# Sinks and sums of two attention steps handled as one item

## The chip, the cores and the metric

The kernel runs on one core of a Trainium2 chip. The metric is the device time of one execution in microseconds (us); lower is better. The engines of the core are TensorE (PE in the profile; PEld is its weight load), VectorE (DVE), ScalarE (ACT), GpSimd (POOL) and SyncE (SP), which issues most of the DMA transfers.

## The reference

Windowed attention with sinks, and a mixture of eight experts behind it, all in fp32.

```python
def _attn_ref(q, k, v, n_sink, window):          # q, k, v: 4 x 8 x 768 x 64
    scores = np.matmul(q, k.transpose(0, 1, 3, 2)) / np.sqrt(D)
    keep = is_sink | in_window                   # the first 4 keys, or 0 <= i - j < 128
    scores = np.where(keep, scores, -1000000000.0)
    a = np.exp(scores - np.max(scores, axis=-1, keepdims=True))
    a = a / (np.sum(a, axis=-1, keepdims=True) + 1e-09)
    return np.matmul(a, v)

def _moe_ref(x, w_gate, w_noise, noise, w1, w2):  # x: 3072 x 512; w1: 8 x 512 x 1024
    noisy = x @ w_gate + np.log1p(np.exp(x @ w_noise)) * noise
    # the two best experts of each token, weighted by a softmax over the two
    for e in range(8):
        out[mask] += top2_w[mask, k, None] * (np.maximum(x[mask] @ w1[e], 0.0) @ w2[e])
```

## The kernel before

The program has two stages. In the attention, a head pair of one batch (16 of them, `g`) is handled in three steps of two query blocks each (`NJ` = 3), so there are 48 steps `n`. A step holds four units `u` (two query blocks, two heads), each a tile of 128 queries by 132 keys: the four sink keys and 128 keys that are put together from the previous and the current block. In the second stage the experts' products run, two chunks of tokens for each expert.

Of a step: `qk` makes the scores in PSUM (ring `S`). `prev` (ACT, L335) copies the previous block's part into the buffer `cbuf`, `cur` (DVE, L342) lays the current block's part over it under a mask. `mins` (DVE, L352) finds the maxima and `minus_max` (DVE, L355) scales them into a bias. ACT exponentiates: in 40 of 48 steps with the sums on the way (`exps_sums`, L366, to which DVE adds 1e-9 in `sums_e`, L374), in 8 without (`exps_bias`, L371, with the sums by DVE in `sums`, L377). `sums_i` (DVE, L385) takes the reciprocals that the routing uses later. `ptr` (TensorE, L405) transposes the window's part, ACT copies it out (`ptr_c`, L408), POOL makes the triangular part (L417), and `pv` multiplies by the values (L431, L434) into a PSUM bank of the ring `X`, which has three.

The sinks go their own way. `pcopy` (ACT at L396 or POOL at L394, 24 steps each) puts the four sink columns of the four units into `pcbuf` rounded, `plow` (POOL, L229, a helper's line) puts the remainder beside them; `pctr` (TensorE, L422) transposes the tile of 128 columns, of which 64 are filled, into the third quarter of the step's `X` bank; `sink_c` (ACT, L438) copies that out; `sinks` (TensorE, L443) multiplies it with the sinks' values, 128 rows deep, the lower 64 of them zeros (`sink_zero`, L288), and adds to the same bank. `pv_c` (ACT, L451) empties the bank, `rows` (DVE, L457) turns the result, and SP writes it to memory.

`logits` (L631 to L647) and `routing` work on a batch when its attention is done, among the steps of the next batch. The gathers and transposes of the first expert's rows (`first_rows`, L982) are placed from step `et` = 38 on.

The order of every engine is made when the program is built: each piece of work is given with an engine, an assumed duration, a priority and what it reads and writes, and `Plan.run` plays them through and issues the instructions in that order. The priorities are numbers in the table `PR`, one for each kind of work with additions for the batch and the head pair. For TensorE a piece whose `kind` (modulo 3) is not that of the piece before is put back by `PR["stay"]`. `ATT` gives the number of buffers of each ring.

Of the kernel before, what the change touches and what calls it, by code (L numbers as in the profile page):

```python
# [9 lines left out]
F32 = mybir.dt.float32  # L10
F32R = mybir.dt.float32r
# [9 lines left out]
PR = dict(cur=-2091.236, cur1=-629.141, cur1_0=-529.244, cur1_9=-69.562, cur_0=50.948, cur_9=251.037, dv=112.004,  # L21
          dv_0=-73.58, dv_9=4.48, exps=21072.868, exps_0=-481.018, exps_9=45.401, ga=631.734, gt=-7.21, lg=-1670.609,
          load_qk=58.212, load_v=5.318, mins=-2643.106, mins_0=509.925, mins_9=12.608, nosink=1.861, nosink_0=479.112,
          nosink_9=248.179, pcopy=-7428.069, pcopy_0=871.282, pcopy_9=8.099, plow=-10376.095, plow_0=29.018,
          plow_9=629.751, prev=0.0, prev_0=-16.085, prev_9=0.012, ptr=58.542, ptr_0=0.38, ptr_9=-305.543,
          ptr_c=-3800.067, ptr_c_0=0.0, ptr_c_9=0.863, ptr_m=-4014.472, ptr_m_0=0.0, ptr_m_9=-30.98, pv=-410.762,
          pv_0=-187.689, pv_9=-878.924, pv_c=-5038.628, pv_c_0=-209.072, pv_c_9=0.0, qk=-4022.153, qk_0=2.321,
          qk_9=-208.172, rows_c=13626.218, rows_c_0=48.694, rows_c_9=136.308, rt=-331.241, sink_c=-108.294,
          sink_c_0=0.0, sink_c_9=415.945, sinks=-317.568, sinks_0=157.442, sinks_9=-760.985, sub=-720.48,
          sub_0=365.118, sub_9=-236.845, sums=-701.98, sums_0=-445.408, sums_9=0.0, sums_i=-169.342,  # L30
          sums_i_0=-1469.516, sums_i_9=200.889, w1=34774.57, pctr_0=0.459, pctr=-982.298, pctr_9=5.399, ga_l=-22.091,
          gt_l=-131.823, ll=1.235, ua=231.313, cur_b0=4741.219, cur_b1=-1045.214, cur_b2=85.388, cur_b3=-83.677,
          cur1_b0=-54.247, cur1_b1=-591.337, cur1_b2=3.535, cur1_b3=-713.751, dv_b0=-1066.109, dv_b1=0.433,
          dv_b2=-102.431, dv_b3=0.8, exps_b0=-674.863, exps_b1=237.689, exps_b2=-678.189, exps_b3=-16.516,
          mins_b0=161.939, mins_b2=688.62, mins_b3=-59.651, nosink_b0=6.061, nosink_b1=276.268, nosink_b2=655.937,
          nosink_b3=-1249.945, pcopy_b0=44.41, pcopy_b1=-154.894, pcopy_b2=-57.297, pcopy_b3=0.905, pctr_b0=470.418,
          pctr_b1=-114.573, pctr_b2=10.539, pctr_b3=155.439, plow_b0=-514.856, plow_b1=-370.826, plow_b2=-377.827,
          plow_b3=141.824, prev_b0=-80.34, prev_b1=837.187, prev_b2=47.509, prev_b3=1019.693, ptr_b0=0.065,
          ptr_b1=-1648.214, ptr_b2=584.948, ptr_b3=103.562, ptr_c_b1=0.65, ptr_c_b2=0.198, ptr_c_b3=426.895,
          ptr_m_b0=-215.003, ptr_m_b2=-0.189, ptr_m_b3=1.114, pv_b0=-199.247, pv_b1=-1.087, pv_b3=-0.137,  # L40
          pv_c_b0=-36.72, pv_c_b1=-168.51, pv_c_b2=0.176, qk_b0=135.717, qk_b1=155.766, qk_b2=1027.551,
          rows_c_b0=10.641, rows_c_b1=13.371, rows_c_b3=-234.252, sink_c_b0=-2240.718, sink_c_b1=-666.896,
          sink_c_b2=-162.853, sink_c_b3=52.344, sinks_b0=2.614, sinks_b1=1736.218, sinks_b2=416.162, sinks_b3=3.919,
          sub_b0=12.389, sub_b1=-711.181, sub_b2=112.247, sub_b3=96.539, sums_b0=-442.042, sums_b2=-0.12,
          sums_b3=-0.52, sums_i_b0=-516.587, sums_i_b1=242.04, sums_i_b2=-207.206, sums_i_b3=-902.581,
          cur_p0=-710.195, cur_p1=5.517, cur_p2=1069.664, cur_p3=0.056, cur1_p0=-301.509, cur1_p1=262.135,
          cur1_p2=92.035, cur1_p3=6.858, dv_p0=-17.962, dv_p1=-239.485, dv_p2=166.849, dv_p3=-462.62, exps_p0=3.095,
          exps_p1=-2398.147, exps_p3=141.316, mins_p0=-35.95, mins_p1=211.786, mins_p2=972.873, mins_p3=-453.475,
          nosink_p0=-0.074, nosink_p1=56.75, nosink_p2=-0.147, nosink_p3=-135.709, pcopy_p0=267.961, pcopy_p1=-69.737,
          pcopy_p2=695.103, pctr_p0=2915.297, pctr_p2=-82.897, pctr_p3=-3.825, plow_p0=332.286, plow_p2=-395.326,  # L50
          plow_p3=163.646, prev_p1=-1397.483, prev_p2=3.465, prev_p3=-1529.655, ptr_p0=1466.062, ptr_p1=-884.904,
          ptr_p2=1086.175, ptr_p3=-2.538, ptr_c_p0=244.684, ptr_c_p1=-219.051, ptr_c_p2=-2381.786, ptr_c_p3=-1767.674,
          ptr_m_p0=-1063.838, ptr_m_p1=-30.78, ptr_m_p2=-2.992, ptr_m_p3=9.279, pv_p0=1767.851, pv_p1=293.164,
          pv_p2=105.005, pv_p3=-913.904, pv_c_p0=-392.431, pv_c_p1=-2.074, pv_c_p2=956.389, pv_c_p3=-1406.214,
          qk_p0=1913.365, qk_p1=316.03, qk_p2=472.316, qk_p3=248.941, rows_c_p0=42.14, rows_c_p1=-1303.087,
          rows_c_p3=4.361, sink_c_p0=705.003, sink_c_p1=-327.727, sink_c_p2=3147.845, sink_c_p3=13.48,
          sinks_p0=-5.891, sinks_p1=-124.688, sinks_p2=-336.715, sinks_p3=-2398.449, sub_p0=-0.186, sub_p1=399.222,
          sub_p2=50.787, sub_p3=-815.066, sums_p1=-47.841, sums_p2=-8.713, sums_p3=2737.503, sums_i_p0=-355.375,
          sums_i_p1=-2009.904, sums_i_p2=-5.004, sums_i_p3=-1209.213, cm_pool=12, gap=3, gap_8=3, dv_pool=4, et=38,
          pc_pool=4, sm_act=10, bias=12, stay=5383.564)  # L60
# [171 lines left out]
def masks(nc, consts, cst, sh, rings):  # L232
# [14 lines left out]
    nc.gpsimd.memset(pcbuf.bitcast(F32), 0.0)  # L247
# [7 lines left out]
ATT = dict(vr=2, vn=2, dv=2, skn=2, sqn=2, kq=3, C=5, mn=3, nb=3, sm=4, ri=2, pc=3, CT=2, CM=2, ps=3, xr=3, S=2, P=1, X=3, xtn=5,  # L255
# [1228 lines left out]
```

## Time and profile before

| | |
|---|---|
| time, median of 3 runs | 773.52 us (772.19 to 774.41) |
| the profiled execution's time | 771.35 us |
| its span | 769.8 us |
| busy in the span: PE, PEld | 739.8 us (96%), 622.6 us (81%) |
| DVE, ACT, POOL | 444.9 us (58%), 349.0 us (45%), 408.2 us (53%) |
| DMA | 97.80 MB, mean 127 GB/s |

The shares of busy time are means over two stages with different limits. The products of TensorE are pipelined, so a busy PE need not be PE at its peak. All times of rows are microseconds from the span's start unless they are marked ns.

### The profile page before, as it was taken

To read this page: it belongs to the slowest core of one execution; us is meant where nothing else is said; L and a number is where in the kernel's file an instruction comes from. 1 tells how busy PE (TensorE), PEld (TensorE's weight loads), DVE (VectorE), ACT (ScalarE), POOL (GpSimd) and SP (SyncE) were. 2 spreads that over 40 slices of the span, in tenths; PEclk is the share of its full clock that TensorE was granted. 3 is DMA by queue.
4 is the path that set the end of the run, shared out by engine and by line. 5 is a ranking of instruction groups with operands and counts; after the bars stand their busy time and mean duration, and the time that the engine had idled before them with its cause. 6 is when DMAs were issued, how large, how long until landed. Compare 5 with 4: busy or idle time off the path is not lost.

```text
span 769.8 us, 12932 instructions
## 1 busy us (share of the span) xinstructions
PE 739.8 (96%) x4499; PEld 622.6 (81%) x4499; DVE 444.9 (58%) x1205; ACT 349.0 (45%) x927; POOL 408.2 (53%) x625
## 2 busy tenths in 40 slices
PE   8899889897999999999999999999999999999995
PEld 4566766575788998889888988898899989999994
DVE  7778898997754555555365446544644474373420
ACT  6889989897313432342334133413332342342221
POOL 6254556867244474728463755557274836547222
PEclk9999999999999999999999999999999999999998
DMA  6448778565561961645164526434452644354133
GB/s 224 138 147 224 173 216 229 184 174 124 144 193 34 261 166 38 153 127 104 31 152 129 106 46 169 130 55 89 141 136 37 153 139 92 67 159 87 24 43 43
DMA packets 58373, 97.80 MB, mean 127 GB/s; under 512 B 19232, under 2 KB 31776, under 8 KB 58304
## 3 DMA queue, kind: packets, MB, share of 16 engines
q1 hardware_dynamic: 44928, 69.34, 30.2%
q0 software_dynamic: 13376, 27.60, 19.9%
q8 instruction: 36, 0.59, 0.3%
q14 instruction: 33, 0.27, 0.1%
HBM read 68.51 MB, written 28.40 MB: 126 GB/s over the span
## 4 chain that ended last, share of the span: by engine, by line
PE 75%; ACT 12%; DVE 7%; issue 4%; POOL 1%; POOLq 0%; ACTq 0%; DVEq 0%
PE H L1075 11%; PE H L1074 11%; PE H L1073 11%; PE Y L1140 11%; PE Y L1141 11%; PE Y L1139 11%; ACT cbuf L366 7%; PE S L332 2%; ACT CT L408 2%; DVE cbuf L342 1%; DVE mn L352 1%; PE Y L1144 1%; PE Y L1145 1%; ACT cbuf L335 1%; PE X L431 1%
## 5 line engine op out<-in xcount | busy, mean ns | idle before, releaser
L927 POOL DMA_INDIRECT xg<-x_rows,rt_idq x174 | 174.7, 1004 | 61.4 <-issue 50.9
L1120 ACT ACTIVATE h<-H 128x384 fp32r<-128x384 f32 (+4 forms) x126 | 63.3, 502 | 267.4 <-PE H L1075 267.3
L1128 DVE SCALAR_TENSOR_TENSOR h<-H,h 128x384 fp32r<-128x384 f32 (+4 forms) x166 | 74.4, 468 | 174.0 <-ACT h L1120 173.3
L1075 PE MATMUL H<-skn,w 128*128 128x384 f32 (+4 forms) x504 | 172.8, 343 | 0.0
L1073 PE MATMUL H<-skn,w 128*128 128x384 f32 (+4 forms) x504 | 172.6, 342 | 0.0
L1074 PE MATMUL H<-sqn,w 128*128 128x384 f32 (+4 forms) x504 | 172.5, 342 | 0.0
L1163 POOL DMA_INDIRECT out<-y,idx x53 | 93.7, 1769 | 50.0 <-ACT y L1148 37.5
L1172 POOL COPY spacer<-h 1x1 f32<-1x1 f32 x88 | 26.5, 301 | 146.2 <-ACT h L1120 145.9
L1073 PEld LDWEIGHTS H<-skn,w 128*128 128x128 f32 x504 | 94.7, 188 | 6.7
L1074 PEld LDWEIGHTS H<-sqn,w 128*128 128x128 f32 x504 | 94.6, 188 | 6.8 <-DVE sqn L229 0.3
L1075 PEld LDWEIGHTS H<-skn,w 128*128 128x128 f32 x504 | 94.5, 188 | 1.9
L1141 PE MATMUL Y<-w2a,h 128*128 128x512 f32 x192 | 75.7, 394 | 0.6 <-DVE h L1128 0.6
L1139 PE MATMUL Y<-w2a,h 128*128 128x512 f32 x192 | 75.0, 391 | 0.7 <-ACT h L1120 0.7
L1141 PE MATMUL Y<-w2b,h 128*128 128x512 f32 x192 | 75.5, 393 | 0.0
L1140 PE MATMUL Y<-w2a,h 128*128 128x512 f32 x192 | 75.5, 393 | 0.0
L1140 PE MATMUL Y<-w2b,h 128*128 128x512 f32 x192 | 75.5, 393 | 0.0
L1139 PE MATMUL Y<-w2b,h 128*128 128x512 f32 x192 | 75.1, 391 | 0.0
L366 ACT ACTIVATE cbuf<-cbuf,nb 128x132 f32<-128x132 f32 x160 | 62.9, 406 | 7.5 <-DVE nb L355 7.3
L332 PE MATMUL S<-kq 64*128 64x264 f32 (+1 forms) x384 | 57.0, 406 | 4.8 <-DVE cbuf L342 3.6
L996 ACT ACTIVATE skn<-xtn 128x512 fp32r<-128x512 f32 (+2 forms) x46 | 27.9, 606 | 62.1 <-DVE xtn L987 62.1
L332 PEld LDWEIGHTS S<-kq 64*128 64x128 f32 x384 | 31.3, 189 | 20.3 <-DVE cbuf L342 9.3
L1141 PEld LDWEIGHTS Y<-w2a,h 128*128 128x128 f32 x192 | 36.0, 188 | 8.7 <-DVE h L1128 1.0
(215 smaller groups left out, 1297.0 us busy)
## 6 DMA issues: line engine op xcount, KB each, us to landing
st<-in_w1l SPq DMA_DIRECT2D x32, 512.0 KB, 4.0
st<-in_w2l SPq DMA_DIRECT2D x32, 512.0 KB, 3.7
kq<-in_kq SPq DMA_DIRECT2D x15, 792.0 KB, 6.8
out<-zt SPq DMA_DIRECT2D x31, 256.0 KB, 5.8
vn<-in_v SPq DMA_DIRECT2D x16, 384.0 KB, 4.5
x_rows<-xr SPq DMA_DIRECT2D x48, 128.0 KB, 3.9
xg<-x_rows,rt_idq POOLq DMA_INDIRECT x174, 2.7
st<-in_vs SPq DMA_DIRECT2D x4, 256.0 KB, 6.4
```

Of the source, the lines that this page charges most:

```text
L332: nc.tensor.matmul(p[:, :2 if j else 1], kq(g)[r, j // 2, 2 + j % 2, NS:], x[:, :2 if j else 1], start=True, stop=True)
L366: nc.scalar.activation(C(n)[:, u], C(n)[:, u], AF.Exp, bias=get("nb", n)[:, u:u + 1], scale=1.0 / math.sqrt(D), accum_out=get("sm", n, [12 ...
L927: nc.gpsimd.indirect_dma_start(out=x[:, i, :], out_offset=None, in_=xbuf.rearrange("r (q d) -> (r q) d", d=sh.SW), in_offset=bass.Indirect ...
L1073: nc.tensor.matmul(p, w[:, 0], xh, start=(i == 0), stop=False)
L1074: nc.tensor.matmul(p, w[:, 0], xl, start=False, stop=False)
L1075: nc.tensor.matmul(p, w[:, 1], xh, start=False, stop=(i == sh.DM // 128 - 1))
L1120: nc.scalar.activation(get("h", FC * q + f, [128, 2 * 128 * FIRST], F32R)[:, :width], H(q, f), AF.Relu)
L1128: nc.vector.scalar_tensor_tensor(h[:, o:o + s1 - s0], p[:, s0:s1], 0.0, h[:, s0:s1].bitcast(F32), op0=OP.max, op1=OP.subtract)
L1139: nc.tensor.matmul(p, hh, w[:, 0], start=(f == 0), stop=False)
L1140: nc.tensor.matmul(p, hh, w[:, 1], start=False, stop=False)
L1141: nc.tensor.matmul(p, hl, w[:, 0], start=False, stop=(f == FC - 1))
L1163: d = nc.gpsimd.indirect_dma_start(out=out, out_offset=bass.IndirectOffsetOnAxis(ap=c["idx"][:size(e, t), e, t:t + 1], axis=0), in_=get("y ...
```

## The change

Steps are taken in pairs, `m` = (2m, 2m + 1). What belongs to a pair is done once, at its second step: `sums_e`, the reciprocals (two where the pair spans two head pairs), `pcopy` and `plow` over eight units, `pctr` over 128 columns that are now all filled, and `sink_c`. The sinks' values lie twice in the tile, in rows 0 to 63 and 64 to 127, by two DMAs, and nothing is filled with zeros; the sinks' products of the first step take the lower half of the rows, those of the second the upper. They, `pv_c` and `rows` of both steps are now placed behind the pair's `sink_c`. Their `kind` is 4 in place of 3, that of the scores modulo 3.

With `bias` = 6 and `turn` below 6, all steps exponentiate with sums and bias; `exps_bias` is gone, and `exps_each`, which would need POOL's subtraction, is not taken. `pcopy` is ACT's in all pairs (`pc_pool` = 0). The rings: C from 5 to 6, sm from 4 steps to 3 pairs, pc and ps from 3 steps to 2 pairs each; `lt` and `lm` of the logits take turns in one buffer. `et` goes from 38 to 42. Assumed durations of some kinds differ, and all priorities of the table are others.

```diff
-          pc_pool=4, sm_act=10, bias=12, stay=5383.564)
+          sums_i_b3=-3046.974, ..., gap=3, bias=6, pc_pool=0, gap_8=3, sm_act=3, dv_pool=4, cm_pool=12, et=42, stay=6134.686)
...
-    nc.gpsimd.memset(pcbuf.bitcast(F32), 0.0)
...
-ATT = dict(vr=2, vn=2, dv=2, skn=2, sqn=2, kq=3, C=5, mn=3, nb=3, sm=4, ri=2, pc=3, CT=2, CM=2, ps=3, xr=3, S=2, P=1, X=3, xtn=5,
+ATT = dict(vr=2, vn=2, dv=2, skn=2, sqn=2, kq=3, C=6, mn=3, nb=3, sm=3, ri=2, pc=2, CT=2, CM=2, ps=2, xr=3, S=2, P=1, X=3, xtn=5,
            lt=1, lm=1, lg=2, H=2)
...
-    def sink_zero(b):
-        nc.gpsimd.memset(get("st", vst[b], [128, 1024], F32, "early")[64:], 0.0)
-
     def sink_values(b):
-        nc.sync.dma_start(get("st", vst[b], [128, 1024], F32, "early")[:64], vss[b])
+        for i in range(2):
+            nc.sync.dma_start(get("st", vst[b], [128, 1024], F32, "early")[64 * i:64 * i + 64], vss[b])
...
-    def sums_e(n):
-        nc.vector.tensor_scalar(get("sm", n), get("sm", n), 1e-9, None, op0=OP.add)
+    def sums_e(m):
+        nc.vector.tensor_scalar(get("sm", m), get("sm", m), 1e-9, None, op0=OP.add)
...
-    def sums_i(n):
-        nc.vector.reciprocal(rib(n), get("sm", n).rearrange("p (a h) -> p a h", a=2))
+    def sums_i(m):
+        n = 2 * m
+        x = get("sm", m)
+        parts = [(n, x.rearrange("p n (a h) -> p (n a) h", a=2))] if n % NJ < 2 and (n + 1) // NJ == n // NJ else [
+            (n + i, x[:, i].rearrange("p (a h) -> p a h", a=2)) for i in range(2)]
+        for i, y in parts:
+            g, jj = divmod(i, NJ)
+            b, pr = divmod(g, HP)
+            r = get("ri", b, [128, NB, H], F32, "tail")[:, 2 * jj:2 * jj + y.shape[1], 2 * pr:2 * pr + 2]
+            nc.vector.reciprocal(r, y)
...
-    def pcs(n, i):
-        t = pcbuf[:, n % plan.rings["pc"], :64].rearrange("p (u x i s) -> p u x i s", u=4, x=2, i=2)
-        return t[:, :, :, i, :], C(n)[:, :, None, :NS].to_broadcast([128, 4, 2, NS])
+    def pcs(m, i):
+        t = pcbuf[:, m % plan.rings["pc"]].rearrange("p (u x i s) -> p u x i s", u=8, x=2, i=2)
+        c = cbuf.rearrange("p c u k -> p (c u) k")[:, 8 * (m % (plan.rings["C"] // 2)):][:, :8]
+        return t[:, :, :, i, :], c[:, :, None, :NS].to_broadcast([128, 8, 2, NS])
...
-    def pctr(n):
+    def pctr(m):
+        x = get("X", XA[2 * m + 1], [128, 4, 128], F32, "ps")
+        nc.tensor.transpose(x[:, 2, :], pcbuf[:, m % plan.rings["pc"], :].bitcast(F32), idf)
...
     def sinks(n):
         b, i = divmod(n // NJ, HP)
+        r = slice(n % 2 * 64, n % 2 * 64 + 64)
         for a in range(2):
-            nc.tensor.matmul(get("X", XA[n])[:, a, :], get("vr", b)[:, a, i].rearrange("p h d -> p (h d)"), get("ps", n),
+            nc.tensor.matmul(get("X", XA[n])[:, a, :], get("vr", b)[r, a, i].rearrange("p h d -> p (h d)"), get("ps", n // 2)[r],
                              start=False, stop=True, skip_group_check=True)
...
+            m, odd = divmod(n, 2)
+            turn = (0, 3, 1, 4, 2, 5)[m % 6]
+            each, bias = turn < PR.get("sm_act", 0), turn < PR.get("bias", 0)
+            if bias:
+                op("DVE", .072, n + .4 + P(g, "sub"), lambda n=n: minus_max(n), r=[("mn", n)], w=[("nb", n)])
+                op("ACT", 1.4, n + .4 + P(g, "exps"), lambda n=n: exps_sums(n), r=[("nb", n)], w=[("C", n), ("sm", m, odd)],
+                   u=[("sm", m)])
...
+            if odd:
+                cs = [("C", n - 1), ("C", n)]
...
+                op(pe, .15 if pe == "ACT" else .33, n + .5 + P(g, "pcopy"), lambda m=m, pe=pe: pcopy(m, pe), r=cs, w=[("pc", m)])
+                op("Pool", .3, n + .5 + P(g, "plow"), lambda m=m: plow(m), r=cs, w=[("pc", m)])
+                op("PE", .11, n + .6 + P(g, "pctr"), lambda m=m: pctr(m), r=[("pc", m)], w=[("X", xa)])
+                op("ACT", .17, n + .6 + P(g, "sink_c"), lambda m=m: sink_c(m), r=[("X", xa)], w=[("ps", m)])
...
+            for i in (n - 1, n) if odd else ():
+                gi, xi = i // NJ, XA[i]
+                op("PE", .22, n + .6 + P(gi, "sinks"), lambda i=i: sinks(i), r=[("ps", m), ("vr", gi // HP)], w=[("X2", xi)],
+                   u=[("X", xi)], kind=4)
+                op("ACT", .27, n + .6 + P(gi, "pv_c"), lambda i=i: pv_c(i), r=[("X2", xi)], w=[("xt", i)], u=[("xtn", gi), ("X", xi)])
...
-    tk, mk = ("lt", li), ("lm", li)
+    tk, mk = ("lt", 2 * li), ("lt", 2 * li + 1)
```

## Rows read from the trace of the kernel before

**Rows 1.** Stages: bounds, length, busy of PE, PEld, DVE, ACT, POOL (count), clock, DMA share, GB/s.

```profile
8.00:193.00 185.00, 165.49 (x1642) 114.93 (x1639) 154.46 (x503) 161.91 (x632) 106.86 (x223) 1.00 0.64 182
...
210.00:700.00 490.00, 490.00 (x2433) 436.84 (x2432) 256.65 (x592) 166.88 (x260) 269.32 (x349) 1.00 0.48 116
```

**Rows 2.** Instructions in time, PE and DVE: start, length, line, operation, idle before.

```profile
193.12 0.48 PE L1073 MATMUL S<-skn,w 128*128 128x512 f32 x1
...
195.63 0.60 DVE L647 TENSOR_REDUCE lg<-lm 128x32 f32<-128x256 f32 x1
200.37 1.29 DVE L1128 SCALAR_TENSOR_TENSOR h<-S,h 128x512 fp32r<-128x512 f32 x2 [4.14 <-ACT h L1120]
```

**Rows 3.** Chain that ended last: whole span by engine, 8 to 193 by line.

```profile
PE 75%; ACT 12%; DVE 7%; issue 4%; POOL 1%; POOLq 0%; ACTq 0%; DVEq 0%
...
by line: ACT cbuf L366 27.2%; ACT CT L408 6.4%; DVE cbuf L342 5.9%; DVE mn L352 5.6%; PE S L332 5.1%; ACT cbuf L335 4.7%; PE X L431 4.4%; issue 3.9%; PE P L405 3.5%; ACT xtn L451 3.1%; PE X L434 3.0%; DVE nb L355 2.5%; DVE xg L972 2.3%; ACT
```

**Rows 4.** ACT in time: one step's exponentials with sums, one without.

```profile
172.89 0.40 ACT L366 ACTIVATE cbuf<-cbuf,nb 128x132 f32<-128x132 f32 x1
...
174.35 0.19 ACT L366 ACTIVATION_READ_ACCUMULATOR cbuf<-cbuf,nb 128x1 f32 x1
...
182.59 1.28 ACT L371 ACTIVATE cbuf<-cbuf,nb 128x132 f32<-128x132 f32 x4
```

**Rows 5.** Groups by line, 0 to 260 us: busy us, mean ns, idle before.

```profile
L229 POOL TENSOR_TENSOR pcbuf<-cbuf,pcbuf 128x32 fp32r<-128x32 f32 x48 | 13.8, 289 | 27.0 <-ACT pcbuf L396 26.0
L422 PE MATMUL X<-idf,pcbuf 128*128 128x128 f32 x48 | 13.8, 301 | 2.7 <-ACT xtn L451 0.9 <-POOL pcbuf L229 0.8 <-POOL pcbuf L394 0.7
L438 ACT ACTIVATE ps<-X 128x128 fp32r<-128x128 f32 x48 | 12.8, 281 | 2.2 <-PE X L434 1.6 <-PE X L422 0.4
L374 DVE TENSOR_SCALAR sm<-sm 128x4 f32<-128x4 f32 x40 | 9.2, 230 | 15.0 <-ACT cbuf L366 14.3
L385 DVE RECIPROCAL ri<-sm 128x4 f32<-128x4 f32 x48 | 8.0, 172 | 0.4
L422 PEld LDWEIGHTS X<-idf,pcbuf 128*128 128x128 f32 x48 | 6.5, 140 | 8.7 <-ACT xtn L451 2.3 <-POOL pcbuf L229 2.0 <-POOL pcbuf L394 1.2
L377 DVE TENSOR_REDUCE sm<-cbuf 128x4 f32<-128x532 f32 x8 | 5.5, 697 | 2.1 <-ACT cbuf L371 2.1
L396 ACT ACTIVATE pcbuf<-cbuf 128x32 fp32r<-128x32 f32 x24 | 5.4, 227 | 0.1
```

**Rows 6.** Pieces of the chain in time, one of each kind: start, us, what.

```profile
12.84 0.16 ACT ps L438
16.17 0.84 DVE sm L374
17.04 0.18 DVE ri L385
...
23.68 0.22 ACT pcbuf L396
...
25.10 0.11 PE X L422
...
45.28 0.68 DVE sm L377
...
46.71 1.30 ACT cbuf L371 x4
```

**Rows 7.** SP in time: the issue of the first sinks' values.

```profile
2.79 0.56 SPq L291 DMA_DIRECT2D st<-in_vs  x1
```

**Rows 8.** The tile X, 8 to 195 us: durations, first and last start; TensorE's waits.

```profile
L443 PE MATMUL X<-ps,vr x96: 272/277/328, 16.0 to 191.2; 128*128 128x128 f32 x96
...
L982 PE MATMUL X<-idf,xg x12: 272/273/328, 156.7 to 169.1; 128*128 128x128 f32 x12
...
  ACT xtn L451: 4.1, 10
```

**Rows 9.** Waits in total, 8 to 193: us, times, longest; the sinks' weight loads.

```profile
PEld X L443 <- issue: 5.1, 17, 0.4
```

More of the change, by code (lines that the diff above doesn't have):

```diff
@@ L20 @@
 BIG = 1.0e30
[L21 to L59, printed above, removed]
-          pc_pool=4, sm_act=10, bias=12, stay=5383.564)
@@ L366, in exps_sums, with exps_each @@
             nc.scalar.activation(C(n)[:, u], C(n)[:, u], AF.Exp, bias=get("nb", n)[:, u:u + 1],
-                                 scale=1.0 / math.sqrt(D), accum_out=get("sm", n, [128, 4])[:, u:u + 1])
-    def exps_bias(n):
+                                 scale=1.0 / math.sqrt(D), accum_out=get("sm", n // 2, [128, 2, 4])[:, n % 2, u:u + 1])
+    def exps_each(n):
         for u in range(4):
-            nc.scalar.activation(C(n)[:, u], C(n)[:, u], AF.Exp, bias=get("nb", n)[:, u:u + 1], scale=1.0 / math.sqrt(D))
@@ L396, in pcopy, with plow @@
             nc.scalar.activation(t, c, AF.Copy)
-    def plow(n):
-        t, c = pcs(n, 1)
-        minus(nc.gpsimd, t, c, pcs(n, 0)[0].bitcast(F32))
+    def plow(m):
+        t, c = pcs(m, 1)
+        minus(nc.gpsimd, t, c, pcs(m, 0)[0].bitcast(F32))
     def ptr(n):
@@ L530, in attention @@
-            pe = "Pool" if n % 8 < PR.get("pc_pool", 0) else "ACT"
-            op(pe, .12 if pe == "ACT" else .23, n + .5 + P(g, "pcopy"), lambda n=n, pe=pe: pcopy(n, pe), r=[("C", n)], w=[("pc", n)])
-            op("Pool", .18, n + .5 + P(g, "plow"), lambda n=n: plow(n), r=[("C", n)], w=[("pc", n)])
-            if not both:
-                op("DVE", .62, n + .8 + P(g, "sums"), lambda n=n: sums(n), r=[("C", n)], w=[("sm", n)])
-            op("DVE", .094, n + .6 + P(g, "sums_i"), lambda n=n: sums_i(n), r=[("sm", n)], w=[("rin", n)], u=[("ri", g // HP)])
+                if each:
+                    op("ACT", 1.19, n + .4 + P(g, "exps"), lambda n=n: exps_each(n), w=[("C", n), ("sm", m, odd)], u=[("sm", m)])
+                else:
+                    op("ACT", .53, n + .4 + P(g, "exps"), lambda n=n: exps(n), w=[("C", n)])
+                    op("DVE", .62, n + .8 + P(g, "sums"), lambda n=n: sums(n), r=[("C", n)], w=[("sm", m, odd)], u=[("sm", m)])
@@ L541, in attention @@
             XA[n] = xa = plan.next("X")
-            op("PE", .11, n + .6 + P(g, "pctr"), lambda n=n: pctr(n), r=[("pc", n)], w=[("X", xa)])
-            op("PE", .87 if jj else .65, n + .6 + P(g, "pv"), lambda n=n: pv(n),
-               r=[("vn", g), ("CT", n), ("dv", g), ("CM", n), ("X", xa)], w=[("X2", xa)], kind=2)
-            op("ACT", .17, n + .6 + P(g, "sink_c"), lambda n=n: sink_c(n), r=[("X", xa)], w=[("ps", n)])
-            op("PE", .22, n + .6 + P(g, "sinks"), lambda n=n: sinks(n), r=[("ps", n), ("vr", g // HP)], w=[("X2", xa)], u=[("X", xa)],
-               kind=3)
@@ new lines, in attention @@
+            op("PE", .87 if jj else .65, n + .6 + P(g, "pv"), lambda n=n: pv(n),
+               r=[("vn", g), ("CT", n), ("dv", g), ("CM", n)] + ([("X", xa)] if odd else []), w=[("X2", xa)], u=[("X", xa)], kind=2)
+            for i in (n - 1, n) if odd else ():
[3 more added lines that the diff above has]
+                op("ACT", .27, n + .6 + P(gi, "pv_c"), lambda i=i: pv_c(i), r=[("X2", xi)], w=[("xt", i)], u=[("xtn", gi), ("X", xi)])
+                op("DVE", .33, n + .7 + P(gi, "rows_c"), lambda i=i: rows(i), r=[("xt", i)], w=[("xrp", i)],
+                   u=[("xr", gi // HP * NJ + i % NJ), ("xtn", gi)])
@@ L549, in attention @@
             b, pr = divmod(g, HP)
-            op("DVE", .33, n + .7 + P(g, "rows_c"), lambda n=n: rows(n), r=[("xt", n)], w=[("xrp", n)],
-               u=[("xr", b * NJ + jj), ("xtn", g)])
-            if pr == HP - 1:
+            for jj in ((jj - 1, jj) if odd and jj else (jj,) if odd else ()) if pr == HP - 1 else ():
+                n = g * NJ + jj
                 plan.dma(n + .7, lambda b=b, jj=jj: rows_d(b, jj), 1.5, r=[("xrp", n - NJ * i) for i in range(HP)],
                          w=[("xrow", b * NJ + jj)], u=[("xr", b * NJ + jj)], n=4)
+            n = m * 2 + odd
@@ L653, in logits @@
     op("PE", .22, z, turn, r=[tk], w=[("X", xa)])
-    op("DVE", .34, z, scale, r=[("X", xa)] + [("rin", n) for n in ns], w=[mk], u=[("ri", b)])
+    op("DVE", .34, z, scale, r=[("X", xa)] + [("rin", n // 2) for n in ns], w=[mk], u=[("ri", b)])
     op("DVE", .5, z, total, r=[mk], w=[("lgs", li)], u=[("lg", b)])
@@ L763, in routing @@
                                get("ri", b)[:, ts, :].rearrange("p t (c a) -> p t a c", a=2)),
-        [("rin", i) for i in range(b * C * (NT // 2), (b + 1) * C * (NT // 2))], ["w"])
+        [("rin", i) for i in range(b * C * NT // 4, (b + 1) * C * NT // 4)], ["w"])
     aux(lambda: s_.tensor_tensor(rt("w")[:, :, 0, :E], rt("wd")[:, 0], rt("wd")[:, 1], op=OP.add), ["wd"], ["w"])
```

78 lines of the change are left out of this document (53 added, 25 removed).

## The prediction

> **What bounds the kernel now.** I read the views from coarse to fine. First the busy time by stage [rows 1]. From 210 to 700 us TensorE is busy for 490.00 of 490.00 us: the expert stage has no gap, so whatever it starts earlier, the end comes earlier by as much. It starts at 193.12 us with the first product of w1 [rows 2]. The attention lies before that, in 185 us from 8 to 193, and there no engine is full: TensorE 165.49, ScalarE (ACT) 161.91, VectorE (DVE) 154.46, GpSimd (POOL) 106.86 us. The granted clock is 1.00 in both stages, so nothing here hangs on the clock.
>
> Then the chain of work that ended last [rows 3]. ACT has 12% of 769.8 us, 92 us, and DVE 7%, 54 us. Nearly all of that must lie in the attention, because later the chain is TensorE's: about half of the 185 us is ACT, a bit over a quarter DVE, the rest TensorE; POOL's 1% is small. Within the stretch one line alone, the exponentials (L366), has 27.2%. So the stage is held by several engines in turn, and a microsecond taken from ACT or DVE counts only where that instruction lies on the chain. That is the reading I use: the pieces of the chain that the change deletes.
>
> **The change part by part.** Everything below is for 48 steps, in the attention alone.
>
> Exponentials. 40 of 48 steps sum while they exponentiate (L366); 8 exponentiate alone (L371) and DVE sums them (L377). The new setting bias=6 is above every value that turn takes, so all 48 go the first way, and the third way, exps_each, is never taken. A step of the first kind lasts from 172.89 to 174.35 + 0.19, 1.65 us; one of the second 1.28 us [rows 4]. ACT pays 8 x 0.37 = +3.0 us, DVE saves 8 x 0.697 = 5.6 us [rows 5].
>
> Shared copies. sink_c runs 24 times in place of 48: ACT saves 24 x 0.281 = 6.7 us. pcopy is all ACT's now, 24 times as before, and twice as wide. 32 columns take 0.227 and 128 columns 0.281 us, so by the line through both 64 columns take 0.245: +0.4 us; the bounds are 0 (the width is free) and +5.4 us (the time doubles) [rows 5]. ACT in sum: 3.0 - 6.7 + 0.4 = -3.3 us of 161.91, 2%.
>
> Sums and reciprocals on DVE. The addition of 1e-9 (L374) runs 24 times in place of 40, -16 x 0.230 = -3.7 us. The reciprocals fall from 48 to 32, since one pair in three spans two head pairs and needs two: -16 x 0.172 = -2.8 us. With the tensor_reduce, DVE: -12.1 us of 154.46, 8%. That 4 or 8 columns make no difference here I take from the reciprocal and the addition being small to begin with; doubled, the rest would cost 24 x 0.230 + 16 x 0.172 = 8.3 us and leave -3.8.
>
> TensorE and POOL. 24 transposes of 0.301 us go (-7.2 us busy, about half of that in a dense stream, where its 0.140 us weight load sets the pace) [rows 5]. The products with the sinks stay at 96, with 64 of 128 rows; their columns stay 128, and I take the time as unchanged. POOL loses its 24 copies and four fills; the remainders (plow) go from 48 x 0.289 us to 24 of twice the width, between 0.289 and 0.578: -6.9 to 0 us. No price for any of it: POOL has 1% of the chain.
>
> What that is on the chain. Of the deleted kinds it holds 17 pieces of sink_c (3.94 us together), 11 of L374 (3.05), 2 of L377 (1.39), 13 of the reciprocal (1.39), 8 of pctr (1.56) and 3 of L371 (3.65); one piece of each stands in [rows 6]. Halved, less 40%, gone, less a third, halved, and 3.65 x 0.37/1.28 added: -1.97 -1.22 -1.39 -0.46 -0.78 +1.06 = -4.8 us. pcopy stands on it with 15 pieces of 2.58 us in all (one stands in that group too); 0.245/0.227 of it adds 0.2. Structure in sum: -4.6 us.
>
> Covers. (a) The sink values are loaded by two DMAs in place of one fill and one DMA. SP needs 0.56 us more before the next key load [rows 7], and for the first batch 256 KB more stand ahead of that load; the values are needed only at the first sinks, 16.0 us [rows 8], and the next keys three steps in. Cost 0; uncovered, 1 to 2 us at the start. (b) et goes from 38 to 42: the first expert's rows are turned four steps later, 4 x 185/48 = 15.4 us. Their turns run from 156.7 to 169.1 [rows 8], hence until 184.5, and 193.12 is when they are needed: 8.6 us of cover. If it were gone each us late would be a us at the end. (c) lt and lm now share one buffer, so the next logits copy waits for the sum before it. The last such sum ends at 196.23 and DVE then idles 4.14 us until the expert's first chunk [rows 2]: up to two such waits of about 1 us are hidden. (d) The last pair's sinks wait for step 47; TensorE has the pv of steps 45 to 47 to do meanwhile. 0, at worst +1.5 us.
>
> **Order anew.** Every priority is different, and no row prices that. It can lose: at most I let it take back the whole gain, +4.6. It can gain: ACT idles 185 - 161.91 = 23.1 us; a third of that regained is -7.7. The middle, 0, is nearest to what the rows say, because the resources that were waited for are the same. Sum: 771.35 - 4.6 = 766.8 for the profiled execution, which lay 2.17 under the median of the runs; on the median 773.52 - 4.6 = 768.9 us.
>
> **A rule against the change.** TensorE's sinks group changes shape, from 128x128 to 64x128. Before, 17 of the weight loads of L443 idled for nothing that the profile shows, 5.1 us, 0.30 us each [rows 9], and I take that for the change of shape in front of them. The transposes have the old shape, the scores (L332) the new one, and pv has 64 columns, so every sinks group between transposes or pv's would change shape twice. The Trainium skill, "TensorEngine Tiling (Array Packing)", Key Properties, says that changing the tiling mode drains TensorE. By the row the sum stays where it is if the groups come to stand beside scores; by the rule each pair that doesn't would pay twice, which is the third rival below.
>
> **The rivals.**
> 1. ACT alone binds. ACT is at 88% of the stage, and L366 is the longest piece. Then DVE's and TensorE's savings are hidden and half (ACT's share of the chain) of -3.3 is left: -1.6, 771.9 us. Against it: DVE's 54 us of chain.
> 2. The pair waits for its PSUM bank (slower). The ring X keeps three banks. The even step's bank is now held until the odd step's sinks are done, a step (3.85 us) longer. Today TensorE waits 10 times, 4.1 us, for L451 to empty one, 0.41 each [rows 8]. If each of 24 pairs waited that at both of its banks, it is 48 x 0.41 - 4.1 = +15.6, with the structure +11.0: 784.5; at one bank 24 x 0.41 - 4.1 = +5.7, 774.6. It decides from 4.6 + 2.3 = 6.9 us of new waits, 0.29 per pair. Against it: the odd step's bank opens with one transpose where two banks did, and 48 steps leave 3 x 3.85 = 11.6 us of bank time each.
> 3. Shape changes: 24 groups x 2 x 0.30 = 14.4, less today's 5.1, +9.3 on TensorE. If all lay on the path, 778.2; with the quarter of the chain that TensorE has, +2.3, 771.2. Slower only if 75% of it is on the path.
> 4. The order regains idle time beyond the structure: -7.7 more, 761.2.
>
> **How the numbers follow.** 0.3% of 773.52 is 2.3 us, about what a measurement of this kernel can tell from no change. Forecast, faster with 764 to 771.2: 0.53. Rival 1, same: 0.18. Rival 2: 0.12, of it 0.02 same. Rival 3: 0.08, half same, half slower. Rival 4, faster: 0.09. Faster 0.53 + 0.09 = 0.62, same 0.18 + 0.02 + 0.04 = 0.24, slower 0.10 + 0.04 = 0.14. The likeliest is 768.9. The range reaches down to 763.5, which leaves out half of rival 4 (0.05), and up to 775.5, which takes in rival 2 at one bank and leaves out its other half and some of rival 3 (0.10).
>
> **What would show it.** Right: the first w1 product without a gap behind it starts near 188.5 instead of 193.1; ACT busy before it falls by 2 to 4 us, DVE by 10 to 13; sink_c, pctr and plow stand at 24, L377's kind is gone; 210 to 700 stays full. Rival 1: DVE falls by that much, its idle time in front of ACT's exponentials grows instead, and the start moves by under 2.3 us. Rival 2: TensorE idles before pv or pctr for the copy of X, more than 4.1 us in all. Rival 3: "issue" idle before the sinks' loads above 5.1 us. The prediction is wrong if the start of the experts moves and the end doesn't (a gap after 210), or if the removed kinds vanish and the waits they hid behind take their place.

## The result and the profile after

The changed kernel takes 762.60 us (median of 4 runs, 761.5 to 764.2) against 772.95 us for the kernel before on the same chip: a ratio of 0.9865, with an interval of 0.9841 to 0.9890. That is 10.4 us less, where 4.6 were predicted, and the time lies under the range. The profiled execution took 761.5 us with a span of 759.9 us.

First the stages of the kernel after: bounds, length, busy time of PE, PEld, DVE, ACT and POOL with their counts, clock, DMA share, GB/s. Its attention ends where the experts start, at 183 us.

```profile
8.00:183.00 175.00, 158.90 (x1614) 113.99 (x1613) 143.21 (x462) 158.49 (x638) 96.64 (x173) 0.99 0.71 195
...
200.00:690.00 490.00, 489.37 (x2430) 436.29 (x2429) 255.78 (x591) 166.61 (x260) 268.40 (x347) 1.00 0.49 115
```

TensorE in time, the start of the experts:

```profile
183.11 0.48 PE L1083 MATMUL S<-skn,w 128*128 128x512 f32 x1
```

Against [rows 1] and [rows 2] the attention shrank from 185 to 175 us and the first product of w1 moved from 193.12 to 183.11, 10.0 us. The experts stay full, and what follows that product takes 759.9 - 183.1 = 576.8 us, against 769.8 - 193.1 = 576.7 before. So the whole gain lies in the attention. There the busy times fell by 3.4 us on ACT, 11.3 on DVE, 6.6 on TensorE and 10.2 on POOL. But the stage fell by three times what ACT lost, and ACT's idle time in it went from 185 - 161.91 = 23.1 to 175 - 158.49 = 16.5 us. This is what has to be explained.

The chain that ended last, after: its shares of the whole span by engine, and by line from 8 to 183 us.

```profile
PE 74%; ACT 13%; DVE 4%; issue 4%; POOL 1%; DMA 1%; SPq 0%; POOLq 0%; DVEq 0%; ACTq 0%
...
by line: ACT cbuf L361 32.2%; ACT CT L408 8.0%; ACT cbuf L330 6.9%; PE X L431 4.9%; PE S L327 4.9%; issue 3.8%; PE X L434 3.3%; ACT xtn L452 3.2%; DVE mn L347 3.2%; DVE cbuf L337 3.1%; PE P L405 2.9%; DVE xr L458 1.8%; PE X L281 1.7%; ACT v
```

Against [rows 3], DVE went from 7 to 4% of the chain and ACT from 12 to 13%; the exponentials alone rose from 27.2% of 185 us, 50 us, to 32.2% of 175 us, 56 us. The stage now hangs on ACT more than it did.

Most of the groups by line of the kernel after that answer to [rows 5], 0 to 250 us: busy us, mean ns, idle time before.

```profile
L361 ACT ACTIVATE cbuf<-cbuf,nb 128x132 f32<-128x132 f32 x192 | 75.6, 414 | 3.8 <-DVE nb L350 3.7
...
L227 POOL TENSOR_TENSOR pcbuf<-cbuf,pcbuf 128x64 fp32r<-128x64 f32 x24 | 8.0, 332 | 23.2 <-ACT pcbuf L396 14.1 <-DVE ri L384 5.4 <-issue 3.6
L422 PE MATMUL X<-idf,pcbuf 128*128 128x128 f32 x24 | 7.3, 305 | 3.0 <-ACT xtn L452 1.4 <-DVE lt L652 1.1 <-DVE nb L350 0.5
L438 ACT ACTIVATE ps<-X 128x128 fp32r<-128x128 f32 x24 | 6.9, 289 | 1.4 <-PE X L434 1.2
L396 ACT ACTIVATE pcbuf<-cbuf 128x64 fp32r<-128x64 f32 x24 | 6.4, 267 | 0.0
```

The counts are the predicted ones: 24 copies, 24 transposes, 24 remainders, 192 exponentials with sums, and in the groups not shown 24 additions and 32 reciprocals. The prices are near: 0.267 us for a copy of 64 columns (predicted 0.245), 0.332 for the remainder (0.289 to 0.578), 0.205 for the wider addition (0.230).

### The profile page after: what moved, and what is told of

It reads as the page before. It is cut to its first block, busy times and chain, and to the rows that moved or that the text cites. A ratio compares the mean times of both kernels' runs of the same rounds, so it can differ in the third digit from the quotient of the medians.

```text
span 759.9 us, 12764 instructions
## 1 busy us (share of the span) xinstructions
PE 732.9 (96%) x4475; PEld 621.5 (82%) x4475; DVE 432.1 (57%) x1165; ACT 346.7 (46%) x935; POOL 395.9 (52%) x572
## 4 chain that ended last, share of the span: by engine, by line
PE 74%; ACT 13%; DVE 4%; issue 4%; POOL 1%; DMA 1%; SPq 0%; POOLq 0%; DVEq 0%; ACTq 0%
PE H L1085 11%; PE H L1084 11%; PE H L1083 11%; PE Y L1151 11%; PE Y L1150 11%; PE Y L1149 11%; ACT cbuf L361 7%; ACT CT L408 2%; ACT cbuf L330 2%; PE S L327 2%; PE X L431 1%; PE Y L1154 1%; PE Y L1155 1%; POOL out L1173 1%; PE X L281 1%
## 5 line engine op out<-in xcount | busy, mean ns | idle before, releaser
L361 ACT ACTIVATE cbuf<-cbuf,nb 128x132 f32<-128x132 f32 x192 | 75.6, 414 | 3.8 <-DVE nb L350 3.7
L417 POOL TENSOR_SCALAR_AFFINE_SELECT CM<-CT 128x512 f32<-128x512 f32 (+1 forms) x48 | 28.8, 602 | 44.4 <-ACT CT L408 44.0
```

## The experiments

Four theories were set against each other. **S**: the work taken out gives nearly all of the gain. **O**: much of it comes from the order made anew and the changed rings (the numbers of buffers). **P**: work is worth what its pieces on the chain that ended last add up to, as the prediction counted. **A**: a microsecond of ACT counts whole in the attention, since ACT is its fullest engine. Each ratio is to the kernel before, measured beside the run on the same chip (medians of 772.8 to 774.0 us); where e3, e4 and e10 are set against the changed kernel's 762.6 us, the two ran on different chips.

**Steps and table crossed.** e1 is the changed kernel with the priorities of the kernel before; e2 is the kernel before with the priorities of the changed one. The settings that aren't priorities (gap, bias, et and so on) stay with the steps.

```diff
-PR = dict(cur=-2882.53, cur1=-977.804, ..., stay=6134.686)
+PR = dict(cur=-2091.236, cur1=-629.141, ..., stay=5383.564)
```

> The changed kernel with the priorities of the table of before (its settings bias, sm_act, pc_pool, et and the assumed durations stay those of the change). Theory S, structure: the whole 10.4 us come from the work taken out and the waits that went with it, whatever the priorities are: 762 to 766 us. Theory O, order: the work taken out is worth the 4.6 us of the sum and the rest is the new priorities: 768 us, or more where the old ones do not fit the pairs.

> The kernel before with the priorities of the new table (its own settings and steps). Theory S: nothing is gained, 772 us or more. Theory O: if the priorities carry over to the old steps, 5 to 6 us are gained, 767 us; if it comes out slower than 774 the table fits its own steps only, and O is neither shown nor ruled out by this run alone.

e1: 772.41 us, ratio 0.9999 (0.9986 to 1.0013). e2: 781.0 us, 1.0096 (1.0079 to 1.0113). The new steps with the old table win nothing, the old steps with the new table lose 8 us. S in its plain form falls: the removed work alone, left to an order that was tuned for other steps, does not show. But a table that doesn't fit costs something by itself, so this doesn't yet say what the order gives. Part of that cost is TensorE's clock. The row of e1 before its experts start, at 195.51 us:

```profile
184.00:196.00 12.00, 11.04 (x71) 7.15 (x68) 4.53 (x11) 2.96 (x8) 3.32 (x5) 0.50 0.39 97
```

The granted clock stood at 0.50 for these 12 us, where [rows 1] has 1.00 for the whole stage; over the span it was 0.981 to 0.992 in the ten runs of e1 and 0.993 to 0.998 in those of the kernel before beside them. So the ratio of 0.9999 doesn't show that the removed work is worth nothing.

**One engine's work put back, order kept.** In e3 to e5 the changed kernel issues its own order, and work that was taken out stands again where its successor stands, as repeated work: e3 does the shared copy twice (24 more on ACT, 6.9 us by their length), e4 puts about 12 us back on DVE (16 additions, 16 reciprocals, 8 reductions of 512 columns), e5 does the 24 transposes twice. In e8, 8 steps exponentiate without sums again and DVE sums them.

```diff
 e3, sink_c
+        for _ in range(2):
             nc.scalar.activation(get("ps", m, [128, 128], F32R), get("X", XA[2 * m + 1])[:, 2, :], AF.Copy)
...
 e4, sums_e
+        if m % 3 < 2:
+            nc.vector.tensor_scalar(get("sm", m), get("sm", m), 0.0, None, op0=OP.add)
+        for _ in range(2 if m % 6 == 5 else 0):
+            nc.vector.tensor_reduce(scratch, m0[:, None, :].to_broadcast([128, 4, 128]), op=OP.add, axis=AX.X)
...
 e4, sums_i
+            for _ in range(2 if len(parts) == 1 else 1):
                 nc.vector.reciprocal(r, y)
...
 e5, pctr
-        nc.tensor.transpose(x[:, 2, :], pcbuf[:, m % plan.rings["pc"], :].bitcast(F32), idf)
+        for i in (3, 2):
+            nc.tensor.transpose(x[:, i, :], pcbuf[:, m % plan.rings["pc"], :].bitcast(F32), idf)
...
 e8, exps_sums and sums_e
+        if n // 2 % 6 == 5:
+            get("sm", n // 2, [128, 2, 4])
+            for u in range(4):
+                nc.scalar.activation(C(n)[:, u], C(n)[:, u], AF.Exp, bias=get("nb", n)[:, u:u + 1], scale=1.0 / math.sqrt(D))
+            return
...
+        if m % 6 == 5:
+            sums(2 * m)
+            sums(2 * m + 1)
+            return
```

> The changed kernel in its own order, with each sink_c run twice: 24 more copies of 0.289 us on ACT, 6.9 us. Theory S, with ACT now almost the bound: most of it comes back, 767 to 769 us. Theory O, by the pieces of the old chain: 2.0 us come back, 764.6 us.

> The changed kernel in its own order, with the work that VectorE lost put back at the sums of a pair: 16 additions, 16 reciprocals, 8 reductions of 512 columns, about 12 us. Theory S: at least 5 us come back, 767.5 us or more. Theory O, by the pieces of the old chain (1.22, 1.39 and 0.46): 3.1 us, 765.7 us.

> The changed kernel in its own order, with the pair's transpose done twice: 24 more transposes of 0.14 us in a stream, 3.4 us on TensorE. Theory P, by the old chain's pieces: 0.8 us slower, 763.4. Theory A, with TensorE's share of the chain unchanged: the same, at most 1 us; 3 us or more would say that TensorE binds with ACT.

> The changed kernel in its own order, with the 8 steps' exponentials without sums again and VectorE's 8 reductions instead: ACT 3.0 us less, DVE 5.6 us more. Theory A: ACT at 1.0, DVE at 0.27 (what the run with DVE's work put back showed), 3.0 - 1.5: 1.5 us faster, about 761. Theory P, by the old chain's pieces: 1.06 off, 1.39 on, 763: no difference.

> The changed kernel itself, beside the next three on one chip, as their base: 762 to 763 us by either theory.

The changed kernel itself took 762.62 us (0.9868) when it was run again beside e5 and e8. The differences from 762.6 are:

| put back | time, us | ratio (interval) | costs | by the chain's pieces |
|---|---|---|---|---|
| e3: 24 copies on ACT | 769.78 | 0.9958 (0.9942 to 0.9975) | +7.2 | +2.0 |
| e4: 12 us on DVE | 765.93 | 0.9914 (0.9885 to 0.9943) | +3.3 | +3.1 |
| e5: 24 transposes | 762.73 | 0.9874 (0.9846 to 0.9903) | +0.1 | +0.8 |
| e8: sums of 8 steps to DVE | 762.31 | 0.9870 (0.9839 to 0.9901) | -0.3 | +0.3 |

P holds for DVE. For the transposes and the exponentials the differences of 0.1 and -0.3 us are too small to tell P from A, since the intervals of these runs are 2 us to either side. For ACT the copies cost far more than P's 2.0. In the windows of e3, one row, and its first product of w1:

```profile
8.00:188.00 180.00, 160.26 (x1618) 114.28 (x1617) 143.32 (x462) 164.67 (x663) 96.60 (x173) 0.99 0.68 191
```

```profile
187.81 0.48 PE L1084 MATMUL S<-skn,w 128*128 128x512 f32 x1
```

ACT's busy time is 6.2 us more than after, the other engines do the same work, and the experts start 187.81 - 183.11 = 4.7 us later. This execution and that of the kernel after had the same granted clock, 0.995; the three other runs of e3 had 0.988 to 0.990 and took 2 to 4 us longer. So with the clock alike the copies cost about 4.7 us, and the 7.2 of the median hold some clock besides; whether the copies themselves bring the lower clock about isn't shown.

Nor are the copies that e3 puts back those that the change took out. Two copies and the next instruction of ACT, in the kernel before and in e3:

```profile
84.95 0.44 ACT L438 ACTIVATE ps<-X 128x128 fp32r<-128x128 f32 x2
85.26 0.61 ACT L408 ACTIVATE CT<-P 128x512 f32<-128x512 f32 x1
```

```profile
64.71 0.59 ACT L439 ACTIVATE ps<-X 128x128 fp32r<-128x128 f32 x2
65.19 0.39 ACT L330 ACTIVATE cbuf<-S 128x264 f32<-128x264 f32 x1
```

ACT's instructions overlap. In the kernel before a copy of 0.28 us lets the next instruction start 0.16 us after its own start (the median of all 48), so 24 copies occupy ACT for 3.8 us and not for 6.7. In e3 the second copy writes the tile that the first writes, and in all 24 pairs it starts 0.03 us behind the end of the first, 0.32 us after its start: 24 of them are 7.6 us. So e3 puts back twice the ACT time that was taken out. The chain has 18 pieces of sink_c, 4.22 us; half of that, 2.1 us for 3.8 us of ACT, is 4.2 for 7.6 (an estimate). That is near the 4.7 us, and P, priced for what e3 really adds, doesn't fail.

**The same ACT work in the old order.** e9 is the kernel before with sink_c done twice in every odd step, 24 more.

```diff
+        for _ in range(1 + n % 2):
             nc.scalar.activation(get("ps", n, [128, 128], F32R), get("X", XA[n])[:, 2, :], AF.Copy)
```

> The kernel before in its own order, with sink_c run twice in the odd steps: 24 more copies of 0.281 us on ACT, 6.7 us. Theory P, the pieces of the chain price ACT's work (as the prediction did): 2.0 us slower, 775. Theory A, a microsecond of ACT counts nearly whole although only a third of the copies lies on the chain, as it did when the copies were put back into the changed kernel: 6 to 7 us slower, 779 to 780.

It took 776.91 us, ratio 1.0071 (1.0040 to 1.0101): +3.7 us by the medians, +5.5 by the ratio. That lies between P's 2.0 and A's 6 to 7. But here too each repeat starts 0.03 us behind the end of its original, so the 24 add 7.4 us of ACT, and the estimate of 4.2 from the pieces lies inside the measured 3.7 to 5.5.

**Equal fit for both.** If a tuned table is part of the gain, both kernels have to be compared with tables that fit them equally well or badly. n has only the settings and no tuned priority; in j1 and j2 each priority of a kernel's own table is multiplied by 1 plus a normal number of spread 0.1, the same for both kernels.

```diff
-PR = dict(cur=-2882.53, ..., stay=6134.686)
+PR = dict(cm_pool=12, gap=3, gap_8=3, dv_pool=4, et=42, pc_pool=0, sm_act=3, bias=6, stay=1.0)
```

> The kernel before with no tuned priorities at all: every kind of work at its step's number, stay 1, own settings. Much slower than 773 by any theory; it is the base of the next run.

> The changed kernel with no tuned priorities either. At equal fit (none) theory S, the pair's work itself: 8 us faster than the run before it (the sum of what came back when parts were put back). Theory O, the new table fits better than the old one did: 5 us or less, or slower.

> The kernel before with each priority of its own table scaled by a random factor (normal, 10%), the same factor for the same name in the next run. Theory O: the fit of a table is worth several us, 776 us or more. If it stays at 773, fit is worth nothing and the change's gain is its work.

> The changed kernel with each priority of its own table scaled by the same factors. Theory S: it loses as much as the kernel before does by it, and the difference stays at 8 to 10 us. Theory O: it loses more, the difference shrinks to 5 us or less.

> The kernel before with its own table scaled by a second set of random factors: near 787 as the first, the base of the next run.

> The changed kernel with its own table scaled by the same second set. Theory S: 8 to 10 us under the run before it. Theory O: 5 us or less under it. A difference far from the 5.5 of the first set would say that single tables scatter too much to tell.

| | before | after | difference |
|---|---|---|---|
| n | 813.28, 1.0508 (1.0464 to 1.0552) | 805.10, 1.0411 (1.0366 to 1.0457) | -8.2 |
| j1 | 787.04, 1.0171 (1.0138 to 1.0204) | 781.54, 1.0093 (1.0058 to 1.0127) | -5.5 |
| j2 | 789.75, 1.0219 (1.0186 to 1.0253) | 775.54, 1.0038 (1.0026 to 1.0050) | -14.2 |

At equal fit the new steps, with their rings and settings, win each time, so they have a gain of their own. Its size can't be read from three pairs that scatter from 5.5 to 14.2 us. What they do show is how much the fit is worth: 10% of noise on a tuned table costs 13 to 19 us, more than the change itself. Part of that is the clock again, 0.981 to 0.993 in the runs of j1 and j2 against 0.992 to 0.998 in those of the kernel before.

**All the work put back.** e10 separates the two in another way: the changed kernel with its own order, rings and priorities, and nearly all removed work in it again, as in e3, e5 and e8 together, with an addition more for each of the 20 pairs that sum on the way, the 16 reciprocals of e4, and two copies of 32 columns on POOL for each pair.

```diff
+        nc.vector.tensor_scalar(get("sm", m), get("sm", m), 0.0, None, op0=OP.add)
...
+        for _ in range(2):
+            nc.gpsimd.tensor_copy(scratch, m0[:, :32])
```

> The changed kernel in its own order and with its own rings, with nearly all of the work put back that the change took out: 24 copies of sink_c on ACT, the 8 steps' exponentials without sums and VectorE's 8 reductions, 20 additions and 16 reciprocals, 24 transposes, 48 small copies on POOL. Theory S, the gain is the work: 772 to 774. Theory O, half is order and rings: 767 to 769.

It took 768.84 us (9 runs), ratio 0.9940 (0.9923 to 0.9957). The windows of e10, of its fastest execution (764.64 us), and its first product of w1:

```profile
8.00:186.00 178.00, 159.52 (x1635) 114.66 (x1634) 151.95 (x501) 161.21 (x627) 105.21 (x221) 1.00 0.68 192
```

```profile
186.67 0.48 PE L1100 MATMUL S<-skn,w 128*128 128x512 f32 x1
```

ACT has 161.21 us, DVE 151.95 and POOL 105.21, within 2% of the 161.91, 154.46 and 106.86 of [rows 1]; TensorE has 159.52, 3.6% under its 165.49. All of it is done in 178 us where the kernel before needs 185. So 773.08 - 768.84 = 4.2 us of the gain by the medians are not work, as theory O had it; the work is worth the rest, 768.84 - 762.62 = 6.2 us. Between the two profiled executions, both with the clock at 1.00 in the whole attention, it is more: the experts start 193.12 - 186.67 = 6.5 us earlier. The split is rough for another reason too: ACT's copies are put back at twice their time, as in e3, and DVE's and TensorE's work not quite in full. And the 4.2 to 6.5 us are not order and rings alone. What e10 repeats, it repeats beside its original, so a pair is still handed from engine to engine once where two steps were handed on twice. No run separates this from the order and the rings.

**Rings alone.** e7 is the kernel before with six score buffers, two for pc and ps and one for lt and lm together; its order is played through anew with these rings and its old priorities.

```diff
-ATT = dict(..., C=5, mn=3, nb=3, sm=4, ri=2, pc=3, CT=2, CM=2, ps=3, ...
+ATT = dict(..., C=6, mn=3, nb=3, sm=4, ri=2, pc=2, CT=2, CM=2, ps=2, ...
...
-    tk, mk = ("lt", li), ("lm", li)
+    tk, mk = ("lt", 2 * li), ("lt", 2 * li + 1)
```

> The kernel before with the changed rings alone: six buffers for the scores in place of five, two for the sinks' copies in place of three, one buffer for lt and lm. Its own table. Theory O, the sixth buffer lets the scores run ahead and regains ACT's idle time: 768 to 771. Theory S: rings give nothing, 772 to 775; slower than that would again be the table's fit.

797.75 us, ratio 1.0334 (1.0294 to 1.0373). Other rings give another order out of the same priorities, and this order is 25 us worse, some of it at the lower clock (0.976 to 0.983 over the span). The run says again how narrow the fit is; it doesn't tell rings from order.

**Further in the direction that pays.** If ACT is the engine whose time counts, the copies of pcbuf belong elsewhere: e11 does them on POOL, at their places in the order. e12 is e11 with e8's exponentials, which takes 3 us more off ACT.

```diff
-... lambda m=m, pe=pe: pcopy(m, pe), r=cs, w=[("pc", m)])
+... lambda m=m: pcopy(m, "Pool"), r=cs, w=[("pc", m)])
```

> The changed kernel in its own order, with pcopy of all 24 pairs moved from ACT to POOL at the same places: ACT 6.4 us less, POOL 6 to 8 us more, and plow no longer waits across engines. Theory A, ACT counts whole in this order: up to 6.4 us faster, 756 to 759. Theory P, pieces of the chain: about 1 us, 761 to 763. Slower than 764 would say that POOL's place for it comes too late for the pair's transpose.

> The run before it and in addition the 8 steps' exponentials without sums, with VectorE's reductions: ACT 9.4 us less, DVE 5.6 more. Theory A: at least as fast as the run before it, 755 to 758. Theory P: 761 to 763.

e11: 760.25 us, 0.9827 (0.9805 to 0.9849). e12: 758.73 us (757.03 to 760.35), 0.9826 (0.9807 to 0.9846), the fastest of all; its experts start at 178.67 us. The windows of e12:

```profile
8.00:179.00 171.00, 156.33 (x1616) 113.18 (x1615) 145.62 (x466) 152.08 (x581) 102.17 (x197) 1.00 0.72 201
```

POOL takes 0.247 us for a copy that took ACT 0.267. The 24 copies bring 2.4 us by the medians (762.62 to 760.25), 2.9 by the ratios. By their length they are 6.4 us, but by the step from their start to the next start, 0.15 us, only 3.6, and ACT's busy time from 8 to 183 us fell by 3.2 (158.49 to 155.32). So a microsecond that ACT is really freed of counts 0.7 to 0.9 here; the 4.7 us of e3 for 7.6, and the 3.7 to 5.5 of e9 for 7.4, are 0.5 to 0.7. With the clock alike A, that it counts whole, is too high each time. The exponentials of e12 add nothing that the ratios show (0.9827 and 0.9826). e12 has 152.08 us of ACT in a stage of 171 us.

## Why the prediction was wrong

**Where it was right.** The gain is in the attention and goes to the end whole, as the full expert stage said. ACT lost 3.4 us (predicted 3.3), DVE 11.3 (12.1). The covers (b) and (c) held at the end of the stage: the first expert's rows are turned from 162.0 to 177.1 us, 6 us ahead of their use at 183.11, and the stage from 200 us on is full. TensorE's waits for X to be emptied and the issue gaps of the sinks' weight loads, two views of 8 to 183 us:

```profile
  ACT xtn L452: 4.9, 11
```

```profile
PEld X L444 <- issue: 1.7, 10, 0.2
```

TensorE waited 11 times for its bank, 4.9 us, against 10 times and 4.1 us [rows 8]: rival 2 falls. The gaps in front of the sinks' loads fell from 5.1 us in 17 to 1.7 us in 10 [rows 9], though their shape changed: rival 3 falls. The rule of the Trainium skill beside it ("TensorEngine Tiling (Array Packing)", Key Properties, that a change of tiling mode drains TensorE) doesn't price these gaps here: counted in the traces, the rows and columns of TensorE's products change 168 times in the attention before and 171 times after, while the gaps fell to a third. What made the gaps is open.

Rival 1 falls with e4: DVE's work, put back, costs 3.3 us, where the rival has DVE's savings hidden. One premise did not carry over: that "nothing here hangs on the clock" is so in the kernel before, but after the change the clock fell to 0.57 from 148 to 152 us, and the nine runs of the changed kernel go from 760.17 us at a granted clock of 0.997 to 766.62 at 0.985.

**The failed step: "Order anew ... The middle, 0".** With the instructions that were taken out running again, the changed kernel is still 4.2 us faster than the kernel before by the medians (e10), 6.5 by the start of the experts in the profiled executions. The step's reason was that "the resources that were waited for are the same". They are not: the ring of the score buffers grew from five to six, and a pair is handed between the engines once where two steps were handed on twice, which no term of the sum prices. Nor does an unchanged amount of work fix the time: with the same steps and rings 10% of noise in the priorities cost 13 to 19 us. The bound of -7.7 held. Rival 4's time of 761.2 us came within 1.4 us of the result, which is in part luck: of the 7.7 us that it gave to the order, 4.2 to 6.5 came.

**The structure, -4.6, isn't shown to have failed.** It measured 6.2 us by the medians of e10, but e10 gives ACT twice the time that the copies took. By the starts of the experts it is 186.67 - 183.11 = 3.6 us, with the clock of the kernel after lower for some 3 us. Term by term: for DVE the pieces were right (3.07 predicted, 3.3 measured). For the exponentials (0.33) and the transposes (-0.78) the runs, at -0.3 and 0.1, are too coarse. For sink_c the prediction counted 17 pieces of 3.94 us where the trace has 18 of 4.22, which makes -2.1 of -1.97. At the 0.5 to 0.9 us per microsecond of ACT that e3, e9 and e11 show, the 3.8 us that were taken out are worth 1.9 to 3.4 us (an estimate), so that -2.1 is at the low end and not far off. Where the prediction erred on ACT is its busy sum: by their lengths the copies save 6.7 us and ACT 3.3, but by the steps from start to start the copies save 3.8, the 32 new reads of sums cost 3.0 (0.093 each) and the wider pcopy 0.7, so that ACT has almost as much to do as before. The busy time fell by 3.4 us even so, near the predicted 3.3; that agreement doesn't confirm the sum behind it.

The parts put back one by one make 7.2 + 3.3 + 0.1 = 10.6 us by the medians, together 6.2; with the 4.7 of e3 at the same clock they make 8.1. In e10 the eight steps without sums give ACT 3.0 us back, which may be the rest; that is argued and not shown. The way matters too: with the old order first, the work taken out gives 0.7 us (773.13 to 772.41, e1, inside its interval and at a lower clock) and the order after it the rest; with the new order first it is 4.2 and then 6.2. Steps and order were made for each other, and a single sum for each isn't a property of the kernel.

**What stays open.** Inside the 4.2 us, the shares of the sixth score buffer (C from 5 to 6), of the priorities and of the hand-overs that a pair saves. e7 couldn't tell, since the order changed with the rings. How much of each difference is the clock that the waits of an order bring about was not separated either. A kernel with six score buffers and the other rings of before was not tried; nor was a table tuned anew for other rings.

## What to carry to other kernels

Price an instruction on a nearly full engine by the step from its start to the next start, not by its length: here 0.16 us against 0.28 for the same copy. The pieces of the chain already hold those steps (0.16 us for a copy in [rows 6]), and as prices they came out right for DVE and near for ACT. When work is put back to test a price, look in the trace whether the repeat runs like the original: here it waited for it and cost twice as much. Compare the granted clock of the executions before a difference is put down to work. Where a change comes with a schedule made anew, give the schedule a term of its own with a range as wide as what a disturbed schedule costs, and test it by putting the work back into the new order, not by exchanging tables. When steps are saved, look at once which of the rest can leave the fullest engine: the copies on POOL gave 2 to 3 us more for one line.

## What the runs showed of the hardware

**One program, two levels of the clock.** Two executions of the changed kernel differ in the start of the experts by 5.0 us, 183.11 and 188.11. The windows of 2 us of the later one, and then of the first:

```profile
170.00:172.00 2.00, 0.84 (x7) 0.55 (x5) 2.00 (x7) 2.00 (x11) 0.66 (x2) 1.00 0.47 63
172.00:174.00 2.00, 0.84 (x7) 0.38 (x5) 1.24 (x4) 2.00 (x10) 1.83 (x3) 0.66 0.91 121
174.00:176.00 2.00, 2.00 (x18) 1.67 (x18) 1.10 (x3) 0.63 (x3) 1.88 (x3) 0.50 0.73 283
```

```profile
172.00:174.00 2.00, 1.41 (x13) 0.96 (x12) 0.26 (x1) 2.00 (x5) 1.78 (x3) 1.00 0.03 11
174.00:176.00 2.00, 2.00 (x42) 1.84 (x39) 0.85 (x5) 1.69 (x3) 1.61 (x2) 1.00 0.00 0
```

In the later execution TensorE was busy for 0.84 of 2 us in two windows running, and the granted clock fell to 0.50, 1.2 GHz, from 174 to 178 us: 18 products in a window where the other execution did 42. In the other, with 1.41 of 2 us, it stayed at 1.00, 2.4 GHz. This is the last of three such stretches in the later execution: the clock is 0.61 from 124 to 128 us, 0.57 from 148 to 156 and 0.57 from 172 to 180, where the other execution has one alone, 0.57 from 148 to 152. Compared by the starts of ACT's copies of X (L452), the later execution is 0.4 us behind at 121 us, 2.0 at 132, 3.2 at 156 and 5.0 at 177. So the 5.0 us arise in these three stretches, and single executions of this kernel are a poor measure.

**VectorE beside GpSimd.** Two instructions of the kernel after, in time, and the group of the second one's line:

```profile
40.68 1.55 POOL L227 TENSOR_TENSOR dv<-vn 128x640 f32<-128x640 f32 x1
...
40.98 2.32 DVE L294 SCALAR_TENSOR_TENSOR vr<-vr,bit,st 128x1024 fp32r<-128x1024 f32 x1
```

```profile
L294 DVE SCALAR_TENSOR_TENSOR vr<-vr,bit,st 128x1024 fp32r<-128x1024 f32 x4 | 6.2, 1543 | 1.2 <-ACT vr L289 1.2
```

The four of L294 take 6.17 us; without this one the other three take 1.28 each. It took 1.04 us more while POOL's subtraction ran for 1.25 us beside it, and it is the longest single instruction on the chain from 8 to 183 us. The Trainium skill, "SBUF — State Buffer", Who interferes with whom, says that a VectorE instruction with two inputs in SBUF contends with a GpSimd instruction that reads SBUF; this pair agrees in direction, and most of the overlap was lost.
